# The second product of blocks 6, 7, 12 and 13 on all 128 rows of the array instead of two halves of 64

## The chip, the core and the metric

The kernel runs on one core of one Trainium2 chip. The metric is the device time of one execution in microseconds (us); lower is better. Five engines of the core appear below: TensorE (PE in the rows, with its weight loads listed apart as PEld), VectorE (DVE), ScalarE (ACT), GpSimd (POOL) and SyncE (SP), which here issues every DMA.

## The reference

A dynamic convolution over 4 x 4096 tokens of width 192 (8 heads, 7 taps whose weights are a softmax), then a feed-forward layer with a hidden width of 2048:

```python
w = softmax(weight_gen)                       # per token and head, over 7 taps
x = einsum('bshk,bskhg->bshg', w, x_unf)      # causal window of 7 tokens
x = x.reshape(16384, 192)
h = x @ w_in                                  # 192 -> 2048
g = where(h >= 1, h, where(h <= -1, 0, (h + 1)**2 / 4))
out = g @ w_out                               # 2048 -> 192
```

All tensors are float32.

## The kernel before

**Tiling.** The 16384 tokens are worked in 32 blocks of 512 tokens, and the hidden width in 16 slices of 128. A step is one block with one slice; the steps of a block are done two at a time, a pair `w` (256 pairs in all, eight to a block). Every float32 operand of a product is split into a high part and a rest of the type fp32r: `hc`, `hl` for the convolved tokens, `whi`, `wlo` for the first weights, `gh`, `gl` for the activated values, and `wo` holds both parts of the second weights, one after the other (2 x 192 columns).

**First product** (`gemm1_pair`, line 378). Its sum runs over 192 = 3 x 64 rows. It is cut into 64-row pieces, and the array is used as two halves: rows 0 to 63 work on the first step of the pair and rows 64 to 127 on the second, at the same time. Nine such twins of 512 columns make a pair.

**Second product** (`gemm2_part`, line 432). Its sum runs over the 128 values of a slice, which would fill the array, but it is cut into two halves of 64 rows as well. A set of 128 tokens (four in a block) has a bank of its own: `o0` holds the banks of sets 0 and 2, `o1` those of sets 1 and 3. In part 0 the upper rows work on one set of a tile and the lower rows on the other; in part 1 they change places, so each bank passes from one half to the other. So that a bank is never written by both, a no-operation on SP (line 441) waits for the last product of a turn, and the first product of the part that takes the bank over waits for that no-operation (`notes`). For each set and step there are two products: `gh` against both parts of `wo` (384 columns) and `gl` against the high part alone (192 columns).

**Order.** The order on each engine is written out by hand: in iteration `w` come `gemm1_pair(w)`, then parts 0 and 1 of the second product of pair `w - 2`, then the activations. `relu`, `square`, `act_g` and `split_g` (ACT and DVE) make `gh` and `gl`; at the end of a block `evac` copies the banks out with ACT (line 456) and DVE (line 457). The convolution of later blocks runs on GpSimd. Transposes through TensorE with full 128-row weights (`turn_sum`, line 267) occur for blocks 0 and 1 only.

Of the kernel before, what the change touches and what calls it, by code (L numbers as in the profile page):

```python
# [10 lines left out]
F32 = mybir.dt.float32  # L11
# [11 lines left out]
def kernel(  # L23
# [21 lines left out]
    nc = tc.nc  # L45
    P = 128
    B, S, D = x.shape
# [5 lines left out]
    NF = DFF // P  # L53
# [8 lines left out]
    n = 4  # L62
# [7 lines left out]
    while groups[-1][-1] + 1 < NB:  # L70
        b = groups[-1][-1] + 1
# [15 lines left out]
    ps_o = ctx.enter_context(tc.tile_pool(name="ps_o", bufs=1, space=bass.MemoryType.PSUM))  # L87
# [10 lines left out]
    wo = const.tile([P, NF, 2, D], F32R, tag="wo", name="wo")  # L98
# [261 lines left out]
    steps = [(b, f) for b in range(NB) for f in range(NF)]  # L360
    NS = len(steps)
    h_t, g_t, o_t = {}, {}, {}
# [43 lines left out]

    notes = []

    def gemm2_part(w, part):


        late = part == 1 and w == NS // 2 - 1
        both = (2 * w, 2 * w + 1)
        order = [(l, turn, i) for l in range(2) for turn in range(n // 2) for i in both] if late else \
            [(l, turn, i) for turn in range(n // 2) for i in both for l in range(2)]
        fresh = set()
        for l, turn, i in order:
            b, f = steps[i]
            note = None
            if turn not in fresh:  # L420
                fresh.add(turn)
                if len(notes) >= n // 2:
                    note = notes[turn - n // 2 if late else -(n // 2)]
            if f == 0 and turn == part == l == 0:

                o_t[b] = [ps_o.tile([P, 2, 512], F32, tag=f"o{m}", name=f"o{m}") for m in range(n // 2)]
            cols = (2 * D, D)[l]
            for h in range(2):
                k = h ^ part
                t = turn + k * n // 2  # L430
                rows = slice(h * Q, (h + 1) * Q)
                mm = nc.tensor.matmul(  # L432
                    out=o_t[b][turn][:, k, 0:cols], lhsT=g_t[i][l][rows, t * P:(t + 1) * P],
                    rhs=wo[rows, f].rearrange("p s d -> p (s d)")[:, 0:cols],
                    start=(f == 0 and part == 0 and l == 0),
                    stop=(f == NF - 1 and part == 1 and l == 1), skip_group_check=True)
                if note is not None:
                    tc.add_manual_dep(mm.ins, note, SYNC, reason="a bank passes to the other rows")
                    note = None
            if i % 2 and l == 1 and not late:  # L440
                nop = nc.sync.nop()  # L441
                tc.add_manual_dep(nop.ins, mm.ins.name, SYNC, reason="matmuls end in order")
                notes.append(nop.ins.name)
        if part == 1:
            for i in both:
                g_t.pop(i)
# [84 lines left out]
    with tc.manual_schedule():  # L531
# [142 lines left out]
        for w in range(NS // 2 + LAGP):  # L674
            i, j = 2 * w, 2 * w + 1
# [4 lines left out]
            if w >= LAGP:  # L680
                gemm2_part(w - LAGP, 0)
                if w == NP - 1:
                    edge_pair(w)
                gemm2_part(w - LAGP, 1)
                pb, pf = steps[j - 2 * LAGP]
                if pf == NF - 1:
                    copies, store = evac(pb)
                    if i < NS:
                        at(w + 1, store, place=0)
# [60 lines left out]
```

## Time and profile before

| | |
|---|---|
| time, median of 2 runs | 1160.93 us (1160.38 and 1161.48) |
| span of the profiled execution | 1158.6 us |
| TensorE busy | 1145.0 us, 99% |
| TensorE weight loads busy | 1038.1 us, 90% |
| ScalarE, VectorE, GpSimd busy | 964.7, 834.1, 792.5 us |

The span runs from the first to the last instruction of one profiled execution, the only one whose instructions are seen; the runs took 1.8 to 2.9 us more than that span, which is what lies around it. Busy time of TensorE is that in which at least one product is under way; products overlap, and their ends are modelled, so it says that the engine never stood still, not that it ran at its peak.

### The profile page before, as it was taken

Reading aid. Unit: us, or ns where it says so; the run is one execution under the profiler, and the core shown is the slowest. Engines: PE = TensorE matmul, PEld = TensorE weight load, DVE = VectorE, ACT = ScalarE, POOL = GpSimd, SP = SyncE. Lnnn points to the kernel's source line nnn. Section 1 sums busy time; section 2 is a strip of 40 time slices with the busy share of each in tenths; the row PEclk is TensorE's granted clock in tenths of the full one; section 3 lists DMA queues with packets and bytes.
Section 4 is the critical chain, followed back from the end, with each engine's and each line's share of the span. In section 5 each row is a group of like instructions: output and inputs, shape, how many; then the busy total and the mean of one; then the engine's idle time right before and its main releaser. Section 6 shows DMA issues by size and latency. Waiting matters only on the chain.

```text
span 1158.6 us, 32197 instructions
## 1 busy us (share of the span) xinstructions
PE 1145.0 (99%) x12885; PEld 1038.1 (90%) x12885; DVE 834.1 (72%) x1271; ACT 964.7 (83%) x1745; POOL 792.5 (68%) x511
## 2 busy tenths in 40 slices
PE   7999999999999999999999999999999999999998
PEld 5799999999999999999999999999999999999997
DVE  8887767677676776767777676776767767677664
ACT  6878888888888888888888888888888888888886
POOL 4788976667857678486686866678576785866310
PEclk9999999999999999999999999999999999999999
DMA  9422222212222212222121222222222122221100
GB/s 229 112 82 79 77 84 90 89 64 73 75 77 90 84 61 82 71 87 90 56 89 59 85 89 90 64 73 74 76 90 95 51 85 70 80 90 57 47 24 15
DMA packets 84052, 91.43 MB, mean 79 GB/s; under 512 B 5056, under 2 KB 75712, under 8 KB 83904
## 3 DMA queue, kind: packets, MB, share of 16 engines
q1 hardware_dynamic: 83904, 89.39, 24.0%
q8 instruction: 101, 1.65, 0.6%
q14 instruction: 47, 0.39, 0.1%
HBM read 64.99 MB, written 24.38 MB: 77 GB/s over the span
## 4 chain that ended last, share of the span: by engine, by line
PE 95%; ACT 2%; DMA 2%; DVE 1%; issue 0%; POOL 0%; DVEq 0%; POOLq 0%; ACTq 0%; SPq 0%
PE o L432 48%; PE psh L378 45%; DMA r<-in_moe_w_in_dram 1%; PE psx L267 1%; DMA r<-in_moe_w_out_dram 1%; PE psx L208 0%; ACT u L392 0%; DVE psh L397 0%; ACT u L389 0%; ACT gh L403 0%; DVE psw L340 0%; DVE gl L404 0%; POOL piece L189 0%; POOL acc L189 0%; ACT hc L258 0%
## 5 line engine op out<-in xcount | busy, mean ns | idle before, releaser
L432 PE MATMUL o<-wo,gh 64*128 64x384 f32 x4096 | 612.2, 355 | 1.5 <-SPq L441 1.4
L397 DVE SCALAR_TENSOR_TENSOR psh<-u,psh 128x512 f32<-128x512 f32 x512 | 354.7, 696 | 299.6 <-ACT u L392 299.4
L432 PE MATMUL o<-wo,gl 64*128 64x192 f32 x4096 | 542.7, 251 | 0.0
L432 PEld LDWEIGHTS o<-wo,gh 64*128 64x128 f32 x4096 | 421.1, 184 | 13.1 <-SPq L441 2.3
L432 PEld LDWEIGHTS o<-wo,gl 64*128 64x128 f32 x4096 | 421.3, 187 | 9.0
L389 ACT ACTIVATE u<-psh 128x512 f32<-128x512 f32 x512 | 301.5, 589 | 93.2 <-PE psh L378 91.2
L404 DVE TENSOR_TENSOR gl<-psh,gh 128x512 fp32r<-128x512 f32 x512 | 345.7, 686 | 15.3 <-ACT gh L403 1.1
L403 ACT ACTIVATE gh<-psh 128x512 fp32r<-128x512 f32 x512 | 299.2, 592 | 65.5 <-DVE psh L397 65.5
L378 PE MATMUL psh<-hc,whi 64*128 64x512 f32 x1536 | 349.8, 404 | 3.7 <-DVE wlo L356 1.9
L189 POOL TENSOR_TENSOR acc<-acc,pr 128x768 f32<-128x768 f32 x185 | 343.8, 1858 | 5.7 <-DVE head L331 2.0
L378 PE MATMUL psh<-hl,whi 64*128 64x512 f32 x1536 | 337.7, 391 | 0.0
L378 PE MATMUL psh<-hc,wlo 64*128 64x512 f32 x1536 | 337.3, 390 | 0.0
L392 ACT ACTIVATE u<-u 128x512 f32<-128x512 f32 x512 | 323.7, 632 | 16.0
L179 POOL TENSOR_TENSOR pr<-x,w 128x768 f32<-128x768 f32 x186 | 286.8, 1549 | 7.1 <-DVE psw L340 7.1
L259 POOL TENSOR_TENSOR hl<-XT,hc 128x512 fp32r<-128x512 f32 x90 | 115.4, 1297 | 221.2 <-ACT hc L258 221.2
L378 PEld LDWEIGHTS psh<-hl,whi 64*128 64x128 f32 x1536 | 173.6, 185 | 34.7 <-DVE hl L259 0.3
L378 PEld LDWEIGHTS psh<-hc,whi 64*128 64x128 f32 x1536 | 173.0, 185 | 29.4 <-DVE wlo L356 4.3
L378 PEld LDWEIGHTS psh<-hc,wlo 64*128 64x128 f32 x1536 | 174.1, 187 | 21.4
L179 POOL TENSOR_TENSOR acc<-x,w 128x768 f32<-128x768 f32 x31 | 47.9, 1547 | 72.5 <-DVE w L155 70.6
L258 ACT ACTIVATE hc<-XT 128x512 fp32r<-128x512 f32 x90 | 55.5, 618 | 0.0
L284 DVE STREAM_TRANSPOSE T<-acc 128x768 f32<-128x768 f32 x30 | 50.9, 1698 | 0.3 <-POOL acc L189 0.3
L457 DVE SCALAR_TENSOR_TENSOR osb<-o,osb 128x384 f32<-128x384 f32 x64 | 32.7, 556 | 2.7 <-ACT osb L456 2.7
(44 smaller groups left out, 188.8 us busy)
## 6 DMA issues: line engine op xcount, KB each, us to landing
x<-in_x_dram SPq DMA_DIRECT2D x28, 960.0 KB
XT<-D SPq DMA_DIRECT2D x180, 128.0 KB
out_dram<-osb SPq DMA_DIRECT2D x31, 384.0 KB
D<-T SPq DMA_DIRECT2D x30, 384.0 KB
x<-in_x_dram SPq DMA_DIRECT2D x4, 945.0 KB
w<-in_weight_gen_dram SPq DMA_DIRECT2D x15, 224.0 KB
r<-in_moe_w_in_dram SPq DMA_DIRECT2D x16, 192.0 KB
r<-in_moe_w_out_dram SPq DMA_DIRECT2D x8, 384.0 KB
```

The source lines that it names most:

```text
L179: held(eng.tensor_tensor(out=t, in0=xtile[:, k:k + n, :].rearrange("p j (h g) -> p j h g", h=H), in1=wt[:, gi, :, :, k:k + 1].to_broadcast ...
L189: held(eng.tensor_tensor(out=o, in0=s, in1=t, op=ALU.add))
L258: ops.append(lambda c=c: nc.scalar.activation(out=hc[:, c], in_=src[c], func=AF.Copy))
L259: ops.append(lambda c=c: lows.append(engines[c].tensor_tensor(out=hl[:, c], in0=src[c], in1=hc[:, c].bitcast(F32), op=ALU.subtract)))
L284: lambda: nc.vector.transpose(out=T.rearrange("p b c j -> p b j c"), in_=acc.rearrange("p j (r b) -> p b j r", b=R)),
L378: nc.tensor.matmul(out=pair[h][:, 0:N], lhsT=l[rows, f // 2, (c + h) % NC if b < 2 else c], rhs=r[rows, c], start=(s == 0), stop=(s == len ...
L389: nc.scalar.activation(out=u_t[i], in_=h_t[i][:, 0:N], func=AF.Relu, scale=0.5 * UNIT, bias=0.5)
L392: nc.scalar.activation(out=u_t[i], in_=u_t[i], func=AF.Square, scale=UNIT ** -0.5)
L397: nc.vector.scalar_tensor_tensor(out=pv, in0=uv, scalar=1.0 / UNIT, in1=pv, op0=ALU.min, op1=ALU.max)
L403: nc.scalar.activation(out=gh[:, 0:N], in_=gv, func=AF.Copy)
L404: nc.vector.tensor_tensor(out=gl[:, 0:N], in0=gv, in1=gh[:, 0:N].bitcast(F32), op=ALU.subtract)
L432: mm = nc.tensor.matmul(out=o_t[b][turn][:, k, 0:cols], lhsT=g_t[i][l][rows, t * P:(t + 1) * P], rhs=wo[rows, f].rearrange("p s d -> p (s ...
```

## The change

A new function `gemm2_whole` does the second product of one step with weights of 128 rows: for each of the four sets of tokens one product of `gh` and one of `gl`, eight products for a step where there were sixteen halves. `gemm2_part` calls it for the pairs of blocks 6, 7, 12 and 13: part 0 does the first step of the pair, part 1 the second. In blocks 6 and 7 `gh` and `gl` alternate set by set; in blocks 12 and 13 the four products of `gh` come first. In these blocks no bank changes rows, and no `notes` are taken or left. Everything else is as it was; what stood at line 432 stands at line 453, and the new products are at line 418.

```diff
+    def gemm2_whole(i, kind):
+
+        b, f = steps[i]
+        if f == 0:
+            o_t[b] = [ps_o.tile([P, 2, 512], F32, tag=f"o{m}", name=f"o{m}") for m in range(n // 2)]
+        order = [(t, l) for t in range(n) for l in range(2)] if kind == 1 else \
+            [(t, l) for l in range(2) for t in range(n)]
+        for t, l in order:
+            cols = (2 * D, D)[l]
+            nc.tensor.matmul(
+                out=o_t[b][t % (n // 2)][:, t // (n // 2), 0:cols], lhsT=g_t[i][l][:, t * P:(t + 1) * P],
+                rhs=wo[:, f].rearrange("p s d -> p (s d)")[:, 0:cols],
+                start=(f == 0 and l == 0), stop=(f == NF - 1 and l == 1), skip_group_check=True)
+
     def gemm2_part(w, part):
...
         fresh = set()
+        whole_rows = {6: 1, 7: 1, 12: 2, 13: 2}.get(steps[both[0]][0], 0)
+        if whole_rows:
+            gemm2_whole(both[part], whole_rows)
+            if part == 1:
+                for i in both:
+                    g_t.pop(i)
+            return
```

On TensorE at the first pair of block 6, before (the two tiles of the block are `o_4276` and `o_4277`; x2 is the twin of two halves, and a row without it is one half):

```order
L378 MATMUL psh<-hl,whi 128x512 x2
L432 MATMUL o_4276<-wo,gh 128x384 [waits SP_sequencer_49,DVE_49]
L432 MATMUL o_4276<-wo,gh 128x384
L432 MATMUL o_4276<-wo,gl 128x192 x2
L432 MATMUL o_4276<-wo,gh 128x384 x2
L432 MATMUL o_4276<-wo,gl 128x192 x2
L432 MATMUL o_4277<-wo,gh 128x384 [waits SP_sequencer_49,DVE_49]
```

The same place now (a row is one product on all 128 rows):

```order
L378 MATMUL psh<-hl,whi 128x512 x2
L418 MATMUL o_4276<-wo,gh 128x384 [waits DVE_49]
L418 MATMUL o_4276<-wo,gl 128x192
L418 MATMUL o_4277<-wo,gh 128x384 [waits DVE_49]
L418 MATMUL o_4277<-wo,gl 128x192
L418 MATMUL o_4276<-wo,gh 128x384
L418 MATMUL o_4276<-wo,gl 128x192
```

The wait for SP is gone, and the second tile, `o_4277`, is first written by the third product of the block and no longer after four twins; ahead of the first product stand half-row ones, as they do after the last.

On TensorE at the first pair of block 12 now:

```order
L378 MATMUL psh<-hl,whi 128x512 x2
L418 MATMUL o_7739<-wo,gh 128x384 [waits DVE_49]
L418 MATMUL o_7740<-wo,gh 128x384 [waits DVE_49]
L418 MATMUL o_7739<-wo,gh 128x384
L418 MATMUL o_7740<-wo,gh 128x384
L418 MATMUL o_7739<-wo,gl 128x192
L418 MATMUL o_7740<-wo,gl 128x192
```

Here the products with 384 columns come four in a row, then those with 192, and the second tile is written by the second product already.

On SP within block 6, before (the no-operations show as waits of the DMA behind them, named PE; `XT`, `D` and `x` are tiles of the convolution, `out_dram` the result):

```order
L281 DMA XT<-D 64x4x128 [waits PE_49,DMAHW7_49]
L281 DMA XT<-D 64x4x128 [waits DMAHW0_49]
L281 DMA XT<-D 64x4x128 [waits PE_49,DMAHW1_49]
L281 DMA XT<-D 64x4x128 [waits DMAHW2_49]
L126 DMA x<-in_x_dram 128x1920 [waits PE_49,Pool_49]
```

The same place now:

```order
L281 DMA XT<-D 64x4x128 [waits DMAHW7_49]
L281 DMA XT<-D 64x4x128 [waits DMAHW0_49]
L281 DMA XT<-D 64x4x128 [waits DMAHW1_49]
L281 DMA XT<-D 64x4x128 [waits DMAHW2_49]
L126 DMA x<-in_x_dram 128x1920 [waits Pool_49]
```

The DMAs keep their order and lose the wait for TensorE; they still wait for what they read and overwrite.

## Rows read from the trace of the kernel before

**Rows 1.** The page: busy time by engine, and the chain by line.

```profile
PE 1145.0 (99%) x12885; PEld 1038.1 (90%) x12885; DVE 834.1 (72%) x1271; ACT 964.7 (83%) x1745; POOL 792.5 (68%) x511
...
PE o L432 48%; PE psh L378 45%; DMA r<-in_moe_w_in_dram 1%; PE psx L267 1%; DMA r<-in_moe_w_out_dram 1%; PE psx L208 0%; ACT u L392 0%; DVE psh L397 0%; ACT u L389 0%; ACT gh L403 0%; DVE psw L340 0%; DVE gl L404 0%; POOL piece L189 0%; POOL acc L189 0%; ACT hc L258 0%
```

**Rows 2.** Waits of TensorE for SP: us in total, times, longest.

```profile
PE o L432 <- SPq L441: 1.4, 1, 1.4
```

**Rows 3.** Busy time of each engine in one block's stretch, block 6.

```profile
246.60:281.70 35.10, 35.10 (x404) 32.66 (x401) 26.72 (x42) 29.92 (x54) 19.78 (x14) 1.00 0.23 76
```

**Rows 4.** Timeline of TensorE's products, one pair: start, us, operation.

```profile
501.12 0.40 PE L378 MATMUL psh<-hl,whi 64*128 64x512 f32 x2
501.36 0.34 PE L432 MATMUL o<-wo,gh 64*128 64x384 f32 x2
501.53 0.25 PE L432 MATMUL o<-wo,gl 64*128 64x192 f32 x2
501.62 0.36 PE L432 MATMUL o<-wo,gh 64*128 64x384 f32 x2
501.82 0.26 PE L432 MATMUL o<-wo,gl 64*128 64x192 f32 x2
...
503.54 0.25 PE L432 MATMUL o<-wo,gl 64*128 64x192 f32 x2
503.63 0.42 PE L378 MATMUL psh<-hc,whi 64*128 64x512 f32 x2
...
505.74 0.34 PE L432 MATMUL o<-wo,gh 64*128 64x384 f32 x2
```

**Rows 5.** Timeline of TensorE's weight loads, the same pair.

```profile
501.54 0.19 PEld L432 LDWEIGHTS o<-wo,gh 64*128 64x128 f32 x2
501.64 0.19 PEld L432 LDWEIGHTS o<-wo,gl 64*128 64x128 f32 x2
501.82 0.19 PEld L432 LDWEIGHTS o<-wo,gh 64*128 64x128 f32 x2
```

**Rows 6.** Timeline of TensorE's products where half-row ones follow full-row transposes.

```profile
14.37 0.49 PE L267 MATMUL psx<-ident,piece 128*128 128x128 f32 x3
14.79 0.50 PE L378 MATMUL psh<-hc,whi 64*128 64x512 f32 x2
...
54.54 0.49 PE L267 MATMUL psx<-ident,piece 128*128 128x128 f32 x3
54.96 0.44 PE L432 MATMUL o<-wo,gh 64*128 64x384 f32 x2
...
57.03 0.49 PE L267 MATMUL psx<-ident,piece 128*128 128x128 f32 x3
57.45 0.44 PE L432 MATMUL o<-wo,gh 64*128 64x384 f32 x2
```

**Rows 7.** Groups of TensorE's instructions: busy us, mean ns of one.

```profile
L267 PE MATMUL psx<-ident,piece 128*128 128x128 f32 x72 | 8.5, 274 | 0.9 <-DVE hl L259 0.5 <-POOL piece L189 0.4
```

**Rows 8.** Timeline of TensorE's weight loads in three early places.

```profile
35.02 0.18 PEld L378 LDWEIGHTS psh<-hc,whi 64*128 64x128 f32 x1 [0.35 <-DVE wlo L356]
...
53.94 0.20 PEld L267 LDWEIGHTS psx<-ident,piece 128*128 128x128 f32 x2 [0.85 <-POOL piece L189]
...
54.96 0.19 PEld L432 LDWEIGHTS o<-wo,gh 64*128 64x128 f32 x2 [0.17 <-issue]
```

**Rows 9.** Timeline of TensorE's products at the first of these places.

```profile
35.03 0.50 PE L378 MATMUL psh<-hc,whi 64*128 64x512 f32 x1
```

**Rows 10.** Timeline of VectorE and TensorE from block 5 to block 6.

```profile
245.46 1.01 DVE L457 SCALAR_TENSOR_TENSOR osb<-o,osb 128x384 f32<-128x384 f32 x2
...
246.60 0.34 PE L432 MATMUL o<-wo,gh 64*128 64x384 f32 x1
...
246.83 0.40 PE L432 MATMUL o<-wo,gh 64*128 64x384 f32 x2
```

**Rows 11.** Waits of SP's queue for TensorE: us in total, times, longest.

```profile
SPq L441 <- PE o L432: 894.9, 1009, 5.2
```

## The prediction, made before the changed kernel was run

> **What bounds the kernel now.** I read the page first: TensorE is busy 99% of the span, and the chain that ends last lies in its two products, 48% in the second and 45% in the first [rows 1]. Next the waits: the only wait of the second product for SP's no-operations is one of 1.4 us [rows 2], and within block 6 TensorE is busy for the whole stretch at a granted clock of 1.00, that is 2.4 GHz, while ACT and DVE have 5 and 8 us to spare in 35.1 [rows 3]. So nothing holds TensorE back in the four blocks; what counts is how long its own stream of products takes there. Last the timeline of one pair [rows 4]: the second product starts at 501.36, the first product at 503.63, the next second product at 505.74. A pair takes 4.38 us, 2.27 of them in the second product: eight twins of gh and gl, at 0.287 each (501.62 to 503.63 are seven).
>
> Inside the 0.287: from gh to gl it is 0.17 where the load of gh's weights had been hidden (501.36 to 501.53, the product lasts 0.34), and 0.20 where it had not (501.62 to 501.82, it lasts 0.36) [rows 4]. The loads tell why: the one for gh starts at 501.54, right behind the start of gl, the next at 501.64, right behind the start of gh [rows 5]. A load needs some 0.11 us, the 192 columns of gl cover only 0.08 of it, and gh stands at the array's door for the rest. So a twin is 0.110 (load) + 0.176 (384 columns and a remainder).
>
> **The change part by part.** It touches 4 blocks of 8 pairs, so 32 pairs.
>
> *The stream itself.* Two halves side by side take 384 + 192 columns, and so does one product on 128 rows; at 2.4 GHz these are 0.160 + 0.080. No full-row product of fp32r is in the trace. The load: a half-row load by itself at 35.02 [rows 8] makes its product last 0.50 [rows 9], 0.11 more than the 0.39 of one whose weights are there (501.12) [rows 4], and two loads at once also take 0.11 (54.96: 0.44 against 0.34) [rows 6, 4]. Twice the rows cost nothing more, so I take 0.11 for 128 rows too, and the 0.08 of gl stay short of the next load. From gh to gl the bounds are 0.160, the bare columns, and the 0.176 of the halves. The nearest rows on 128 rows are the transposes, 0.11 apart (three in 0.49, of which one lasts 0.274 [rows 6, 7]), which leaves no remainder beside a load of 0.11, so they speak for the low end; the halves of the same type speak for the high one, and I take the middle, 0.168. So a set and step costs 0.27 to 0.286, taken as 0.278, against 0.287: eight of them save 0.01 to 0.14 us a pair, taken as 0.07. The order of blocks 12 and 13 has the same sum: four gh at 0.168 with their loads hidden, four gl at 0.110.
>
> *The switch of the array from halves to whole and back*, twice a pair, 64 times in all. Three places show full-row products followed by half-row ones [rows 6]: the last transpose's modelled end is at 14.86, 55.03 and 57.52, and the next load starts at 14.79, 54.96 and 57.45, each time 0.07 earlier. One of them is marked as waiting for nothing the profile shows, 0.17 us [rows 8], and 0.20 from the last product's start is the same in all three though the work is not. The load is then not hidden: the first product lasts 0.44 for 0.34, 0.50 for 0.39. On the way back after gl (lasts 0.25) the load starts 0.18 after it, and the first product runs 0.29 after it; now that is 0.11 (503.54 to 503.63, and the 0.42 for 0.39 that follows). Cost 0.18. On the way in no row shows it (where transposes follow half-row products, a wait for data hides it); taken as the same rule, after hl (0.39) the load starts at 0.32, the first gh at 0.43, now 0.23. Cost 0.20, bounds 0 and 0.20. Together 0.38 a pair.
>
> The Trainium skill, "TensorEngine Tiling (Array Packing)", section Key Properties, says that changing the tiling mode drains TensorE, whichever way. It speaks against this change; the three places agree for the way back, no row shows the way in, and by the page the sum keeps its 0.20.
>
> *The waits.* The notes cost TensorE nothing in these blocks [rows 2], so their going gives nothing. SP spends 894.9 us waiting on such no-operations [rows 11]; without them its DMAs may go earlier, each still behind what it reads and overwrites, and no product waits for them now: nothing either way. The banks: DVE is through with block 5's at 246.47, block 6 starts at 246.60 [rows 10]; the second tile is now wanted 0.16 to 0.27 after that start and not 0.57, still later than 246.47, and the start itself moves back by the switch: nothing. In block 6 one half runs 0.23 behind the other (246.60, 246.83) [rows 10]; the first switch has to wait for the later one, once, within rounding.
>
> *Sum*: 0.38 - 0.07 = 0.31 us a pair, bounds 0.24 and 0.37, times 32 pairs: 9.9 us, 7.7 to 11.8. All of it is on the path that sets the end. The profiled execution's span would go from 1158.6 to 1168.5; the 2.3 us between span and median stay, so the time is 1160.9 + 9.9 = **1170.8 us**, with 1168.6 to 1172.7 on this mechanism, +0.8%. About 2% (23 us) is what the verdict takes as a change, so this is "same".
>
> **The rivals.**
>
> *A. Weights of 128 rows load faster.* Two full-row loads stand in 0.20, each of 0.14: the second starts 0.06 after the first [rows 8], so a load there takes some 0.055. Then gl goes at its columns, 0.088 (501.53 to 501.62), a set costs 0.25 to 0.264, eight save 0.18 to 0.30, and the way in costs 0.05 less: 0.33 - 0.24 = 0.09 a pair, 2.9 us (1 to 5): 1164. Against it: these are transposes of plain float32, and fp32r loads take 0.11 whether one or two run. The skill's "TensorE: Matmul & The Clock Gate", section LDWEIGHTS, has a load go by its columns and not its rows, 128 columns in 107 ns; by that, A falls.
>
> *B. Only the way back drains.* The load for the first gh then hides under hl as today, and the pair loses 0.18 - 0.07 = 0.11: 3.5 us (1 to 6), 1164. For it: nothing shows the way in. Against it: the weights of 128 rows need both halves of the array at once. A and B together: 0.18 - 0.24 = -0.06 a pair, 1159.
>
> *C. Slower by far: full rows stream at half rate.* The only full-row float32 products here, the transposes, take 0.11 for 128 columns [rows 6, 7], some 1.2 columns per ns, and their load of 0.055 doesn't explain it. If fp32r on 128 rows goes so too, a set costs 0.32 + 0.16 and not 0.287: 8 x 0.19 = 1.5, and the switches 0.38, 1.9 us a pair, 61 us: 1222, +5%. It decides from 0.73 us a pair, a set of 0.33. Against it: the halves take fp32r at the full rate, and a transpose passes float32 through unrounded, which is other work.
>
> *D. A dearer switch.* The way in has two halves to empty, each with its own end, and full loads behind them; 0.35 each way makes 0.62 a pair, 20 us: 1181.
>
> **How the numbers follow.** Forecast 0.56, A 0.10, B 0.13, A with B 0.03, C 0.09, D 0.09. The range 1161 to 1177 holds the forecast with its bounds, nearly all of A and B, and the cheaper half of D: 0.8. Slower by over 2% are C and a sliver of D: 0.10. Faster by over 2% would need 0.73 us a pair saved out of 2.27, for which there is no row: 0.01. Within 2%: 0.89.
>
> **What the changed profile would show.** Gaps or late loads at both borders of line 418 in all 32 pairs, some 0.2 us each; the first gh lasting 0.43 to 0.45; gh to gh 0.27 to 0.29 in blocks 6 and 7; gl to gl 0.11 and gh to gh 0.16 to 0.18 in blocks 12 and 13; a pair of 4.6 to 4.75 us there, 4.39 elsewhere; no new waits. I am wrong if gl follows gl at 0.09 (A), the first gh comes 0.23 after hl (B), gh to gl takes 0.3 (C), or a border costs clearly more than 0.2 (D).

## The result and the profile after

The changed kernel takes 1172.38 us (1172.27 and 1172.48) where the kernel before took 1160.93: 11.45 us more, a ratio of 1.0097 with a 95% interval of 1.0067 to 1.0126. Its profiled execution spans 1170.4 us, 11.8 more than before. The forecast was 1170.8, with 1168.6 to 1172.7 for its own mechanism and 1161 to 1177 with the rivals.

The page's busy times and its chain by line, which answer to [rows 1]:

```profile
PE 1156.4 (99%) x12373; PEld 1034.3 (88%) x12373; DVE 834.5 (71%) x1271; ACT 966.2 (83%) x1745; POOL 792.6 (68%) x511
...
PE psh L378 45%; PE o L453 41%; PE o L418 7%; DMA r<-in_moe_w_out_dram 2%; PE psx L267 1%; ACT u L392 1%; ACT u L389 0%; DVE psh L397 0%; DMA x<-in_x_dram 0%; ACT gh L403 0%; SPq L281 0%; DVE psw L340 0%; DVE gl L404 0%; POOL piece L189 0%; POOL acc L189 0%
```

TensorE is busy for 11.4 us more with 512 fewer products, while no other engine's busy time has grown by more than ScalarE's 1.5: the loss is inside TensorE's stream. Its waits for SP are two where there was one, and the second is 0.2 us long and lies far behind the four blocks (line 462 is the no-operation of old line 441; [rows 2] has the one of before):

```profile
PE o L453 <- SPq L462: 1.6, 2, 1.4
```

The stretch of block 6, whose answer of before is [rows 3]:

```profile
246.96:285.04 38.08, 38.08 (x274) 31.38 (x273) 27.06 (x43) 30.01 (x54) 20.30 (x13) 1.00 0.23 72
```

The clock is 1.00 as before, TensorE is busy throughout, and eight pairs take 38.08 us where they took 35.10: 4.76 us a pair for 4.387, so 0.373 more, and 32 times that is 11.9 us. One pair on TensorE in the timeline, which answers to [rows 4]:

```profile
256.15 0.40 PE L378 MATMUL psh<-hl,whi 64*128 64x512 f32 x2
256.48 0.44 PE L418 MATMUL o<-wo,gh 128*128 128x384 f32 x1
256.76 0.25 PE L418 MATMUL o<-wo,gl 128*128 128x192 f32 x1
256.85 0.36 PE L418 MATMUL o<-wo,gh 128*128 128x384 f32 x1
...
258.76 0.25 PE L418 MATMUL o<-wo,gl 128*128 128x192 f32 x1
258.94 0.50 PE L378 MATMUL psh<-hc,whi 64*128 64x512 f32 x2
...
260.91 0.40 PE L378 MATMUL psh<-hl,whi 64*128 64x512 f32 x2
261.24 0.44 PE L418 MATMUL o<-wo,gh 128*128 128x384 f32 x1
```

And its weight loads, beside [rows 5]:

```profile
256.47 0.19 PEld L418 LDWEIGHTS o<-wo,gh 128*128 128x128 f32 x1 [0.36 <-issue]
256.58 0.19 PEld L418 LDWEIGHTS o<-wo,gl 128*128 128x128 f32 x1
256.76 0.19 PEld L418 LDWEIGHTS o<-wo,gh 128*128 128x128 f32 x1
...
258.94 0.19 PEld L378 LDWEIGHTS psh<-hc,whi 64*128 64x128 f32 x2 [0.16 <-issue]
```

Three things are to be seen. On the way in, the first gh follows hl after 0.33 us and not 0.23. Its load starts only with it (0.36 of waiting for nothing the profile names), and so it lasts 0.44 and not 0.34: 0.43 in all, 0.20 more than before. On the way out, the next load starts 0.18 after gl, where it was 0.09, and the product lasts 0.50 where it lasted 0.42 [rows 4]: 0.17 more. In between, from gl at 256.76 to gl at 258.76 are seven sets in 2.00 us, 0.286 each, against 0.287: the whole products are no faster than the halves. The two ends together are 0.37, the whole of the loss.

The late load on the way in comes in all 32 pairs. The waits of TensorE's loads name nothing for 21 of them and ScalarE's gh for 8:

```profile
PEld o L418 <- issue: 7.7, 21, 0.4
PEld o L418 <- ACT gh L403: 2.9, 8, 0.4
```

In the timeline the idle time is 0.36 or 0.37 in each of the 32, whatever is named, so it is not ScalarE that the load waits for.

In blocks 12 and 13, where the four gh come first, the timeline of one part is this (merged where they follow each other):

```profile
482.20 0.40 PE L378 MATMUL psh<-hl,whi 64*128 64x512 f32 x2
482.53 0.97 PE L418 MATMUL o<-wo,gh 128*128 128x384 f32 x4
483.33 0.59 PE L418 MATMUL o<-wo,gl 128*128 128x192 f32 x4
483.76 0.54 PE L418 MATMUL o<-wo,gh 128*128 128x384 f32 x2
```

From the first gh of part 0 to the first of part 1 it is 1.23 us, of which 0.11 is the first load; the 1.12 left is about the 4 x 0.286 = 1.14 of the other order, and gh follows gh at 0.18 ((0.97 - 0.44) / 3). Block 12's eight pairs also take 38.08 us, as its stretch shows:

```profile
463.49:501.57 38.08, 38.08 (x275) 31.87 (x273) 27.30 (x43) 30.16 (x54) 20.50 (x14) 1.00 0.22 72
```

### The profile page after: what moved, and what is told of

Its sections match the earlier page's. It is cut to its first block, busy times and chain, and to the rows that moved or that the text cites. A ratio compares the mean times of both kernels' runs of the same rounds, so it can differ in the third digit from the quotient of the medians.

```text
span 1170.4 us, 31009 instructions
## 1 busy us (share of the span) xinstructions
PE 1156.4 (99%) x12373; PEld 1034.3 (88%) x12373; DVE 834.5 (71%) x1271; ACT 966.2 (83%) x1745; POOL 792.6 (68%) x511
## 4 chain that ended last, share of the span: by engine, by line
PE 93%; DMA 2%; ACT 2%; DVE 1%; issue 0%; SPq 0%; POOL 0%; DVEq 0%; POOLq 0%; ACTq 0%
PE psh L378 45%; PE o L453 41%; PE o L418 7%; DMA r<-in_moe_w_out_dram 2%; PE psx L267 1%; ACT u L392 1%; ACT u L389 0%; DVE psh L397 0%; DMA x<-in_x_dram 0%; ACT gh L403 0%; SPq L281 0%; DVE psw L340 0%; DVE gl L404 0%; POOL piece L189 0%; POOL acc L189 0%
## 5 line engine op out<-in xcount | busy, mean ns | idle before, releaser
L453 PE MATMUL o<-wo,gh 64*128 64x384 f32 x3584 | 532.7, 355 | 1.6 <-SPq L462 1.6
L453 PE MATMUL o<-wo,gl 64*128 64x192 f32 x3584 | 469.1, 251 | 0.0
L453 PEld LDWEIGHTS o<-wo,gh 64*128 64x128 f32 x3584 | 359.3, 184 | 11.8 <-SPq L462 2.3
L453 PEld LDWEIGHTS o<-wo,gl 64*128 64x128 f32 x3584 | 361.5, 187 | 8.5
L378 PE MATMUL psh<-hl,whi 64*128 64x512 f32 x1536 | 326.6, 391 | 0.0
L378 PE MATMUL psh<-hc,wlo 64*128 64x512 f32 x1536 | 326.1, 390 | 0.0
L378 PEld LDWEIGHTS psh<-hl,whi 64*128 64x128 f32 x1536 | 163.9, 185 | 35.2 <-DVE hl L259 0.3
L378 PEld LDWEIGHTS psh<-hc,wlo 64*128 64x128 f32 x1536 | 164.3, 186 | 21.9
L418 PE MATMUL o<-wo,gh 128*128 128x384 f32 x256 | 68.9, 362 | 0.0
L418 PEld LDWEIGHTS o<-wo,gh 128*128 128x128 f32 x256 | 44.9, 188 | 11.7 <-issue 7.7
```

The lines of the kernel that those rows point to most:

```text
L378: nc.tensor.matmul(out=pair[h][:, 0:N], lhsT=l[rows, f // 2, (c + h) % NC if b < 2 else c], rhs=r[rows, c], start=(s == 0), stop=(s == len ...
L418: nc.tensor.matmul(out=o_t[b][t % (n // 2)][:, t // (n // 2), 0:cols], lhsT=g_t[i][l][:, t * P:(t + 1) * P], rhs=wo[:, f].rearrange("p s d ...
L453: mm = nc.tensor.matmul(out=o_t[b][turn][:, k, 0:cols], lhsT=g_t[i][l][rows, t * P:(t + 1) * P], rhs=wo[rows, f].rearrange("p s d -> p (s ...
```

## The experiments

The theory: the loss is the array's change from halves to whole and back, a fixed 0.37 us for a pair's two changes, whatever is done in between. Halves or whole is called the array's cut below, and a place in the stream where it changes a border. Rivals: full-row products are dear by themselves (0.37 for eight sets), or SP's queue, which no longer waits for TensorE in these blocks, does harm.

**Half as many changes, the same products.** In the changed kernel the second products of two pairs are done together, behind two first products:

```diff
-                gemm2_part(w - LAGP, 0)
...
-                gemm2_part(w - LAGP, 1)
+                p = w - LAGP
+                joined = steps[2 * p][0] in (6, 7, 12, 13)
+                for q in ([p - 1, p] if p % 2 else []) if joined else [p]:
+                    gemm2_part(q, 0)
...
+                    gemm2_part(q, 1)
```

> As the changed kernel, but in blocks 6, 7, 12 and 13 the second products of two pairs are done together, after every second first product, so there are 32 changes of the array's cut instead of 64 and the same 512 full-row products. Theory (the loss is the changes of cut, 0.37 us for a pair's two): half of it stays, 16 x 0.37 = 6 us, 1167 us. Rival (the loss goes with the full-row products themselves): the loss stays at 11 to 12 us, 1172 us. Second rival (the pace of SP without its waits): also 1172 us. A risk for all: two first products in a row may wait for their banks; then the joined halves of the next run show it too.

The same edit in the kernel before is its control.

> The control of the run before it: the kernel before, with halves everywhere and the second products of two pairs of blocks 6, 7, 12 and 13 done together. No cut changes, so all theories expect 1161 us if joining costs nothing by itself; what it costs above that is to be taken off the joined full-row run.

Measured: 1171.99 us with whole products, 1167.56 with halves, against 1160.48 for the kernel before on the same chip (ratios 1.0099, 1.0082 to 1.0116, and 1.0062, 1.0047 to 1.0077). By its total the first run speaks for the rivals; by its control it doesn't. Joining costs 7.1 us by itself: the second of two first products waits for its banks, as the waits of TensorE's loads show. With halves:

```profile
PEld psh L378 <- DVE gl L404: 7.1, 15, 0.7
```

With whole products:

```profile
PEld psh L378 <- DVE gl L404: 5.8, 13, 0.8
```

What whole products add to joined halves is 1171.99 - 1167.56 = 4.4 us, not the 11.5 of the changed kernel, and less than the 6 expected; but the four runs of the control lie between 1166.50 and 1170.15, so 6 is not excluded. Where no bank is waited for, the timeline gives the price of one excursion:

```profile
250.15 0.44 PE L418 MATMUL o<-wo,gh 128*128 128x384 f32 x1
...
254.91 0.50 PE L378 MATMUL psh<-hc,whi 64*128 64x512 f32 x2
...
259.29 0.44 PE L418 MATMUL o<-wo,gh 128*128 128x384 f32 x1
```

From one start of the second products to the next it is 9.14 us for two pairs, against 2 x 4.387 = 8.77 before: 0.37 for two pairs, where the changed kernel pays 0.75. So the loss goes with the changes and not with the products. In the two profiled executions the spans differ by 4.8 (1169.4 and 1164.6), still less than 16 x 0.37. Their timelines show where some of it went. From the start of a pair's first product to that of the second pair after it, the joined kernels take 9.14 and 8.78 us where neither waits for a bank, but 9.55 and 9.39 in the third such turn of block 6, where TensorE's load waits for gl, 0.36 us with whole products and 0.65 with halves: part of the change falls into that wait.

**The changes without the change.** The kernel before, with its halves and notes, gets one more product per pair of the four blocks, with weights of zero, once on full rows at the pair's end and once as a twin of halves in part 1:

```diff
+    def extra(w):
+        b, f = steps[2 * w]
+        if b not in (6, 7, 12, 13):
+            return
+        nc.tensor.matmul(
+            out=o_t[b][0][:, 0, 0:D], lhsT=zr, rhs=wo[:, f, 0],
+            start=False, stop=False, skip_group_check=True)
```

> The kernel before with all its halves and notes, and one product more for each pair of blocks 6, 7, 12 and 13, at the pair's end: 128 rows, 192 columns, weights of zero, added to a bank of the block. Theory (changes of cut): in and out of the full cut, 0.18 to 0.20 each, and 0.08 to 0.11 for the product, 0.46 us a pair, 14.8 us in 32 pairs, 1176 us. Rival (full-row products are dear by themselves, by 0.37 for eight of them): 0.11 + 0.05 a pair, 5 us, 1166 us. Second rival (SP's pace): as for a plain product, 3.5 us, 1164 us.

> The same extra work as a twin of halves (64 rows each, 192 columns, weights of zero), within part 1 of the pair, so that the cut never changes. Theory: only the twin's own time, one load's 0.11 us a pair, 3.5 us, 1164 us; the difference to the full-row extra product, 11 us, is the two changes of cut. Rival (any product more costs that much): 1176 us like the other.

Measured: 1180.35 and 1169.70 us against 1160.48 (1.0168, 1.0153 to 1.0183; 1.0077, 1.0062 to 1.0092). Both came out some 5 us too high, for a reason of my own making: the zeros were made by GpSimd and handed to ScalarE in one place, ScalarE stood still behind GpSimd's queue (4.8 us at once in the first), and one pair took 9.2 and 9.5 us in place of 4.4. The difference, 10.7 us, is as expected. Both were repeated with the zeros made earlier:

> The kernel before with one extra full-row product (192 columns, weights of zero) at the end of each pair of blocks 6, 7, 12 and 13, as before, but with the zeros made in two steps far apart, so that no engine stands still for them (that cost 4.8 us once in the first two of these kernels). Theory (changes of cut): 32 x 0.46 = 14.7 us, 1175 us. Rival (full-row products are dear by themselves): 5 us, 1166 us.

> The same with the extra product as a twin of halves in part 1, zeros made early. Theory: a load's 0.11 to 0.12 us a pair, 3.5 to 3.8 us, 1164 us. Rival (any extra product costs as much as the full one): 1175 us.

Measured: 1175.32 us (1.0129, 1.0114 to 1.0144) and 1164.31 us (1.0030, 1.0018 to 1.0041) against 1160.45: 14.9 and 3.9 us, both as the theory had them. The timeline of the first at such a product:

```profile
269.06 0.25 PE L432 MATMUL o<-wo,gl 64*128 64x192 f32 x2
269.24 0.36 PE L458 MATMUL o<-wo,zr 128*128 128x192 f32 x1
269.52 0.50 PE L378 MATMUL psh<-hc,whi 64*128 64x512 f32 x2
```

One full-row product among halves costs 0.465 us a pair (14.9 / 32), the same product as halves 0.12: the two changes cost 0.34 here, where all eight sets are halves, the notes are kept and SP waits for TensorE as before (915.1 us in all, 894.9 in [rows 11]). That ends both rivals.

**All blocks.** The same change in blocks 2 to 30:

```diff
-        whole_rows = {6: 1, 7: 1, 12: 2, 13: 2}.get(steps[both[0]][0], 0)
+        whole_rows = 1 if 2 <= steps[both[0]][0] <= 30 else 0
```

> The changed kernel with the full-row second product in all blocks from 2 to 30 (29 blocks, 232 pairs), gh and gl alternating. Theory (a fixed 0.373 us for each pair that changes the cut twice): 232 x 0.373 = 86.5 us, 1247 us. Rival (the loss belongs to something of the first pairs of a block, or to the borders between the two kinds of block, of which there are four in the changed kernel and two here): it grows by less, 1166 to 1230 us. Rival (other engines fall behind when it goes on for long): more than 1260 us.

Measured: 1245.80 us against 1160.85 (1.0728, 1.0710 to 1.0746): 84.9 us for 232 pairs, 0.366 each, and in the timeline 231 of these pairs take 4.76 us. Each pair pays the same; it is no matter of the places where the two kinds of block meet.

**The products by themselves.** At the end of the kernel before, runs of products whose results nobody uses:

```diff
+        for _ in range(16):
+            whole(512)
...
+        for _ in range(8):
+            whole(512)
+            twin(512)
```

> The kernel before, and at its end runs of products whose results nobody uses, for their spacing in the trace alone: 16 of each of full-row fp32r with 512, 384, 256 and 192 columns, full-row bf16 with 512, twins of halves with 512, upper halves alone with 512; then eight times a full one followed by a twin (512), by an upper half alone (512), and by a twin with 192 columns. Theory on the size of a product: full rows and twins have the same spacing, 0.23, 0.174 and 0.11 for 512, 384 and 192, and an idle lower half changes nothing. On the remainder over columns at 2.4 GHz: if it is a share (fp32r streams at some 2.2 columns per ns) 256 come at 0.116 and bf16 at 0.216; if it is a fixed time that a load under way costs, 256 come at 0.123 and bf16 at 0.23. On the change of cut: each border of the alternating runs costs 0.18 to 0.20 over the plain spacing (with 192 columns: over 0.11), the upper half alone like the twin; if only the change from full to half drains, every second border comes at the plain spacing.

Only its spacings are read. The timeline, with equal products merged; the rows are of the separate runs, full rows first, then bf16, then the upper half alone:

```profile
1154.77 4.00 PE L458 MATMUL bank<-wo,gh 128*128 128x512 f32 x16
...
1158.78 2.63 PE L458 MATMUL bank<-wo,gh 128*128 128x384 f32 x14
...
1161.54 1.82 PE L458 MATMUL bank<-wo,gh 128*128 128x256 f32 x14
...
1163.52 1.61 PE L458 MATMUL bank<-wo,gh 128*128 128x192 f32 x13
...
1165.08 3.63 PE L469 MATMUL bank<-ident 128*128 128x512 bf16 x16
...
1172.70 2.96 PE L462 MATMUL bank<-wo,gh 64*128 64x512 f32 x12
```

A row runs from the first start to the last end, so the spacing is its length without one product's own, over the count less one: (4.00 - 0.50) / 15 = 0.233 for 512 columns (0.50 for one, since the first waits for its load), (2.63 - 0.34) / 13 = 0.176 for 384, (1.82 - 0.28) / 13 = 0.118 for 256, (1.61 - 0.27) / 12 = 0.112 for 192, where the load sets the pace, and (2.96 - 0.39) / 11 = 0.234 for one half with 512. So fp32r takes 0.455 to 0.461 ns a column at 512, 384 and 256, on full rows and on half rows alike: the remainder is nearer to a share of the columns than to a fixed time. For bf16 it is (3.63 - 0.39) / 15 = 0.216.

The alternating runs, a full product and a twin with 512 columns, and a full product and the upper half alone:

```profile
1176.29 0.50 PE L458 MATMUL bank<-wo,gh 128*128 128x512 f32 x1
1176.72 0.50 PE L462 MATMUL bank<-wo,gh 64*128 64x512 f32 x2
1177.15 0.50 PE L458 MATMUL bank<-wo,gh 128*128 128x512 f32 x1
...
1184.07 0.50 PE L458 MATMUL bank<-wo,gh 128*128 128x512 f32 x1
1184.49 0.49 PE L462 MATMUL bank<-wo,gh 64*128 64x512 f32 x1
1184.91 0.50 PE L458 MATMUL bank<-wo,gh 128*128 128x512 f32 x1
```

0.43 and 0.42 from one to the next where equal ones follow at 0.233: 0.19 to 0.20 for each border, in both directions, with one half idle too. With 192 columns, in the next run, it is 0.28 to 0.29 where equal ones follow at 0.112, so 0.17 for a border, in the two places before the clock fell (last section).

**What counts as another cut.** A second set of runs at the end of the kernel before, two kinds in turn:

```diff
+        for _ in range(8):
+            whole16()
+            twin16()
...
+        for _ in range(8):
+            whole(512)
+            part(96, 128)
```

> The kernel before, and at its end more runs of products nobody uses, for their spacing alone: 16 twins with 384 columns; then eight times two kinds in turn, 512 columns each: bf16 full and bf16 twin; fp32r full and bf16 full; fp32r full and fp32r with 96 rows; fp32r full and fp32r with weights of 64 columns; upper half and upper half with weights of 64 columns. Theory (the array's cut is what drains): borders of the first kind cost as in fp32r less what a bf16 load is shorter by, some 0.1 to 0.2; changing the type alone costs nothing (spacing 0.22 to 0.235); 96 rows need the full cut, nothing; weights of 64 columns are another cut, 0.2 a border, or nothing if only rows count. Rival (any change of shape or type drains): all of them cost 0.1 to 0.2 a border. Twins with 384 columns come at 0.175 like full rows.

Its 16 twins and four of its alternating runs in the timeline: bf16 full and twin, full fp32r and full bf16, fp32r with 128 and 96 rows, fp32r with weights of 128 and 64 columns:

```profile
1154.15 3.00 PE L462 MATMUL bank<-wo,gh 64*128 64x384 f32 x32
...
1157.40 0.39 PE L477 MATMUL bank<-ident 64*128 64x512 bf16 x2
1157.72 0.39 PE L469 MATMUL bank<-ident 128*128 128x512 bf16 x1
...
1163.03 0.39 PE L469 MATMUL bank<-ident 128*128 128x512 bf16 x1
1163.07 0.58 PE L458 MATMUL bank<-wo,gh 128*128 128x512 f32 x1
1163.49 0.39 PE L469 MATMUL bank<-ident 128*128 128x512 bf16 x1
...
1166.48 0.40 PE L458 MATMUL bank<-wo,gh 128*128 128x512 f32 x1
1166.72 0.39 PE L472 MATMUL bank<-wo,gh 96*128 96x512 f32 x1
1166.95 0.40 PE L458 MATMUL bank<-wo,gh 128*128 128x512 f32 x1
...
1171.14 0.39 PE L458 MATMUL bank<-wo,gh 128*128 128x512 f32 x1
1171.37 0.39 PE L472 MATMUL bank<-wo,gh 128*64 128x512 f32 x1
1171.60 0.39 PE L458 MATMUL bank<-wo,gh 128*128 128x512 f32 x1
```

One load of the bf16 twins:

```profile
1157.39 0.10 PEld L477 LDWEIGHTS <-ident 64*128 64x128 bf16 x2 [0.23 <-issue]
```

The twins come at (3.00 - 0.34) / 15 = 0.177, the full rows' 0.176. 96 rows or 64 weight columns among full products cost nothing, 0.23 as always, and neither do 64 weight columns among upper halves, the fifth run; a change of type costs at most 0.01 for two borders (full bf16 and full fp32r in turn come at 0.46 the two, 0.45 by themselves). Between full and half rows bf16 pays 0.10 a border (0.32 for 0.216), half of what fp32r pays: the other half of fp32r's 0.20 would be its weight load of 0.11, which a change of cut brings into the open (its products last 0.50 at each border, those of bf16 0.39 as always). The loads of bf16 are late as well, but last 0.10 in the trace where those of fp32r last 0.19, which fits; no run separates the load from the rest. Only the change between full rows and halves counts, of what was tried.

No version that beats the kernel before came out of these runs.

## Why the prediction was right

**What bounds the kernel**: as read. TensorE's stream is the path, no wait of more than 0.2 us was added to it, and no other engine's busy time moved by more than 1.5 us.

**The change of the array's cut**: right in place and size. Forecast 0.18 out and 0.20 in; the trace of after shows 0.17 and 0.20. The way out was taken from rows of the same event, the way in only from its likeness, with no row of before to show it; the benches with both directions at 0.19 to 0.20 confirm it. The rule of the Trainium skill that was weighed there ("TensorEngine Tiling (Array Packing)", section Key Properties, that a change of mode drains TensorE) agrees with the trace in both directions: the load behind a border starts 0.32 us after hl (256.15 to 256.47) and 0.18 after gl (258.76 to 258.94), both times 0.07 to 0.08 before that product's modelled end, where within the sets the load for gh starts together with the gl ahead of it (256.76).

**The stream**: this is the term that was mis-sized. Forecast a saving of 0.07 us a pair (0.01 to 0.14), measured 8 x 0.001, nothing: the mid value between the bare columns and the halves was wrong, the end taken from the halves right. The step that failed reads the transposes as a sign that full rows leave no remainder; in the benches the remainder goes with the type (0.46 ns a column for fp32r, 0.42 for bf16), not with the rows. With no saving and the 0.17 of the way out the sum is 0.37 a pair, 11.8 us, the growth of the span; so a pair takes 4.76 us, a little over the 4.6 to 4.75 of the signs, and the time lies near the upper end of the mechanism's range.

**The waits, the banks, SP**: nothing, as forecast. SP now waits elsewhere (in blocks 6 and 7 57.3 us for VectorE's transposes, where it had waited 56.3 for TensorE) and TensorE doesn't notice.

**The rivals**: A falls, since the load of full rows takes the 0.11 of a half (256.47 to 256.58), B since the way in drains, C since 512 columns on full rows take 0.233 and not 0.43, D since a border costs 0.2 and not 0.35.

## What to carry to other kernels

Before a piece of TensorE's stream is put on other rows of the array than its neighbours, count the borders: each cost 0.2 us with fp32r weights and 0.1 with bf16 here, and a saving inside the piece has to exceed that. Two halves of 64 rows side by side ran as fast as one product on 128 rows, so a sum that would fill the array may as well stay cut in halves where its neighbours are. Where borders can't be avoided, fewer and longer pieces pay less, if the banks allow it: here joining two pieces cost about what it saved (1171.99 us against the changed kernel's 1172.38).

## What was not expected of the hardware

fp32r products come at 0.46 ns a column, on full rows and in halves alike, where bf16 ones on full rows come at 0.42; why is open. The Trainium skill, "TensorE: Matmul & The Clock Gate", section Back-to-back issue gap, gives columns over 2.4 GHz and 2.5 ns as the gap of an isolated warm product, and a smaller one, some 131 ns at 512 columns, for a sustained stream of loads and products. The streams here are not that fast: bf16 comes at 0.216 us, the first figure, and fp32r at 0.233, 8% above it, and the measurement decides.

The last run of the first bench, full products and twins of 192 columns in turn, began at 0.28 us from one to the next; between 1189 and 1191 us the granted clock fell to the lower level, 1.2 GHz, where it stayed to the end of the products. The stretches of its trace:

```profile
1180.00:1189.00 9.00, 9.00 (x26) 3.89 (x25) 0.00 (x0) 0.00 (x0) 0.00 (x0) 1.00 0.00 0
1189.00:1191.00 2.00, 2.00 (x9) 1.05 (x8) 0.00 (x0) 0.00 (x0) 0.00 (x0) 0.94 0.00 0
1191.00:1197.00 6.00, 5.88 (x20) 3.59 (x20) 0.00 (x0) 0.00 (x0) 0.00 (x0) 0.50 0.00 0
```

The same turns with 512 columns just before kept 1.00, and so did the changed kernel, whose products between two borders take over 2 us. TensorE counts as busy throughout (the last product ends within the last stretch), so its busy share gave no warning. What in these turns made the clock fall was not tested.
